# Attention sums kept in DRAM with 32 rows a head, and a resident bias

## The chip, the cores and the metric

The kernel runs on one core of a Trainium2 chip. The time is the device time of one launch in microseconds (us), and lower is better. Times before and after are medians of several runs on a chip; the rows further down are from one execution that the hardware profiler recorded.

## The reference

Two transformer layers are applied to x of 2048 tokens by 640 channels. Both layers share one set of weights. Each layer is attention with 32 heads of 20 channels over a sliding window of 256 tokens, and then a feed-forward block with a squared ReLU.

```python
def _A_ref(x, wqkv, wo):
    H = 32; Dh = D // H; W = 256
    q, k, v = split(x @ wqkv)                      # each head: 2048 x 20
    scores = jnp.einsum("bhqd,bhkd->bhqk", q, k) * (Dh ** -0.5)
    mask = (idx[:, None] - idx[None, :] >= 0) & (idx[:, None] - idx[None, :] < W)
    p = _softmax(jnp.where(mask, scores, -1e9))
    return merge_heads(jnp.einsum("bhqk,bhkd->bhqd", p, v)) @ wo

def _B_ref(x, w1, b1, w2, b2):
    r = jnp.maximum(x @ w1 + b1, 0)
    return (r * r) @ w2 + b2

for _ in range(2):
    x = x + _A_ref(_layernorm(x), A_wqkv, A_wo)
    x = x + _B_ref(_layernorm(x), B_w1, B_b1, B_w2, B_b2)
```

## The kernel before

**Units.** The tokens are cut into groups of T = 256, so that two layers make 16 units u = 0 to 15. A unit has these steps. The layer norm makes y, which is turned to channels on partitions. `stage_qk` and `stage_v` make queries, keys and values (each float32 product is three float16 products of high and low halves, `mm3`, line 339). The attention of the unit runs over eight quads of four heads. `stage_o` multiplies the divided sums by wo and adds them to x, a second layer norm follows (its y goes through TensorE transposes in unit 0 and in the last units, line 403, else through DMA transposes), and `stage_f` is the feed-forward block.

**A quad.** `max_quad` computes scores into the PSUM banks bb (line 703) and reduces them to row maxima on VectorE (lines 717, 720). `exp_quad` computes the scores again with the maxima subtracted (line 840), ScalarE takes the exponentials into pt (line 825, four of them for a quad), and GpSimd and VectorE clear the masked corners (lines 854, 863). `pv_quad` multiplies pt by the values into the tile pv and a spare piece of bb (line 931). ScalarE and VectorE bring both to the tile ot (lines 943, 946). Values carry a 21st column of ones, so each head has 20 rows of sums and one of the softmax's denominators. A quad's four heads stand at partitions 0, 32, 64 and 96 of ot.

**The way through DRAM.** After every second quad ot, which holds two quads, is written to a DRAM tile o (line 951). When a unit's eight quads are written, `load_o` reads the denominators as rs (each row four times, line 984) and the sums as val (line 985; the tiles are called od, or ov in the last two units). In four quarters of 64 tokens, VectorE takes the reciprocal of rs (line 1017) and multiplies (1020), ScalarE rounds to float16 (1024), VectorE makes the rest (1027). `stage_o` uses the result.

**The order of the work.** Nothing is scheduled by the compiler: each engine runs its own list in order. A planner in the kernel writes the lists. It keeps a clock for each engine (A is ScalarE, D VectorE, G GpSimd, S the DMA queue of SyncE), gives each posted job a cost in ns and a priority, and puts it into a list when its inputs should be ready by those costs. Dense products (`stage_qk`, `stage_v`, `stage_o`, `stage_f`) fill TensorE between the steps of the quads. Costs of DMAs thus decide where on VectorE and ScalarE the jobs behind them stand. Weights are loaded from ScalarE's queue during unit 0 and the start of unit 1 (`load_wo`, `load_w1`, `load_w2`), and split to high and low by `convert` (lines 271 and 272).

**The bias b2.** In each unit `add_b2` loads b2, spread over 128 partitions, into one of the two buffers of the pool xt (line 1069), and four additions on GpSimd add it to the unit's x (line 1076, two for each of two row blocks of 128 tokens). The layer norm of unit u + 2 loads its rows into the same pool, and waits for these additions.

Of the kernel before, what the change touches and what calls it, by code (L numbers as in the profile page):

```python
# [10 lines left out]
F32 = mybir.dt.float32  # L11
# [3 lines left out]
ALU = mybir.AluOpType  # L15

P = 128
Q = P // 2
S = 2048
D = 640  # L20
F = 1536
H = 32
DH = 20
NL = 2
T = 256
NG = S // T
NU = NL * NG
KC = D // P
# [17 lines left out]
def kernel(ctx: ExitStack, tc: tile.TileContext, x, wqkv, wo, w1, b1, w2, b2, out):  # L46
    nc = tc.nc
# [3 lines left out]
    sb = ctx.enter_context(tc.tile_pool(name="sb", bufs=1))  # L51
# [30 lines left out]
    for h in range(2):  # L82
        nc.gpsimd.tensor_copy(drop[h * Q:(h + 1) * Q], edges[h * Q:(h + 1) * Q, :, h * Q:(h + 1) * Q])
    b1s = sb.tile([P, FC], F32, name="b1s")
    kts = []
    for i in range(3):
        kts.append(sb.tile([P, NP, T], F16, name=f"kt{i}"))
# [18 lines left out]
    def set_row(i, k):  # L106
        nc.vector.memset(krow[i][:, 512 * k:512 * (k + 1)], PAIR)
# [45 lines left out]
    def bulk(fn, size, *deps, **kw):  # L153

        return post("A", 400.0, fn, *deps, prio=2, size=size, idle=True, land=WLAND, **kw)

    def dma(fn, size, *deps, n=1, cost=450.0, prio=1, **kw):

        return post("S", n * cost, fn, *deps, prio=prio, size=size, **kw)
# [107 lines left out]
    gate, gate0, gate2 = [Job("S", 0.0, None, [], 0.0, 0) for i in range(3)]  # L267
# [25 lines left out]

    def load_wo():

        v = wo.rearrange("(h c d) n -> d h c n", c=KC, d=4)
        raw = w2raw[:, (FC - KC) * D:].rearrange("p (c n) -> p c n", n=D)
        loads = []
        for d in range(4):
            loads.append(bulk(lambda d=d: nc.scalar.dma_start(raw[d * H:(d + 1) * H], v[d]), H * KC * D * 4, gate0))  # L300
        for c in range(KC):
            woj[c] = convert(raw[:, c], wo_s[:, 0, c], wo_s[:, 1, c], D, loads[-1], *loads[:-1])
        rowset[1] = [post("D", 460, lambda k=k: set_row(1, k), prio=2) for k in range(4)]
# [499 lines left out]
    ods, ots = {}, {}  # L803
# [103 lines left out]
    def pv_quad(n, quad):  # L907
        u, qd = divmod(n, NQ)
        boxes, masks = quad
        need(*pvfree)  # L910
        pvfree.clear()
        to, jobs = mm_tile([P, T], "pv")
        spare = bb6[1][:, 2, T:]
        pv = [to, spare]
        halves = quarters(u)
        for k in range(4 if halves else 2):
            need(*masks[k // 2 if halves else k])
            for j in range(2):
                for e in range(2):
                    jj = 2 * j + e  # L920
                    c = (4 * qd + jj) * (DH + 1)
                    for h in range(2 if halves else 1):
                        kb = ORDER[h][k] if halves else 2 + k
                        vf = vts[(2 * (u if kb >= 2 else u - 1) + kb % 2) % 6][1]
                        if halves:
                            o, q0, w = PARTS[h][kb]
                            r, a, b = slice(h * Q, (h + 1) * Q), (10 * j + o) * Q, (10 * j + o + w) * Q
                        else:
                            q0, w = 2 * k, 4 - 2 * k
                            r, a, b = slice(0, P), 512 * k + w * Q * j, 512 * k + w * Q * (j + 1)  # L930
                        nc.tensor.matmul(pv[h][32 * jj:32 * (jj + 1), q0 * Q:(q0 + w) * Q], vf[r, c:c + 32],  # L931
                                         boxes[e]["pt"][r, a:b], start=(k == 0), stop=(k == (3 if halves else 1)),
                                         skip_group_check=True, tile_position=(h * Q, 32 * jj))
            now[0] += (440.0, 225.0, 330.0, 305.0)[k] if halves else 420.0
        apart[0] = True
        if qd == 0:
            ods[u] = tc.dram_tile([DH + 1, H, T], F32, name=f"o{u}")
        if qd % 2 == 0:
            ots[u] = sb.tile([P, 2, T], F32, name="ot", bufs=2)
        ot = ots[u]  # L940

        def out():
            nc.scalar.copy(ot[:, qd % 2], to)  # L943

        def both():
            nc.vector.tensor_tensor(ot[:, qd % 2], spare, ot[:, qd % 2], op=ALU.add)  # L946

        def write():
            drv = ods[u].rearrange("d (q j) n -> j d q n", j=4)
            for j in range(4):  # L950
                nc.sync.dma_start(drv[j][:, qd - 1:qd + 1, :], ot[32 * j:32 * j + DH + 1])

        jobs.append(post("A", 262, out, prio=0))
        tops()
        done = jobs[-1]
        if halves:
            done = post("D", 330, both, done, prio=urgency["turn"])
            pvfree.append(done)
        if qd % 2:
            ojobs[u, qd] = dma(write, 4 * (DH + 1) * 2 * T * 4, done, n=4, cost=350.0)  # L960

    ojobs, stored, waiting = {}, [], {}

# [2 lines left out]
    ols = {}  # L966
    opened = Job("S", 0.0, None, [], 0.0, 0)

    def load_o(u, late=False, free_=()):
# [3 lines left out]
        if late:  # L973
            val = sb.tile([P, KC, T], F32, name="ov", tag="qt", bufs=2)
            od = sb.tile([P, KC, 2, T], F16, name="od", tag="yT", bufs=1)
        else:
            raw = sb.tile([P, 2, KC, T], F32, name="od", tag="hh", bufs=1)
            val = raw[:, 0]
            od = raw[:, 1].rearrange("p c n -> p (c n)").bitcast(F16).rearrange("p (c a n) -> p c a n", a=2, n=T)
        wrote = [ojobs.pop((u, qd)) for qd in range(1, NQ, 2)]  # L980
        rs = sb.tile([P, T], F32, name="rs", bufs=1)

        def load():
            nc.sync.dma_start(rs, ods[u][DH:].to_broadcast([4, H, T]))
            nc.sync.dma_start(val, ods[u][:DH].rearrange("(c d) h n -> (d h) c n", d=4))

        loaded = dma(load, P * (KC + 1) * T * 4, *wrote, *free_, n=2, prio=0)
        if u == NU - 1:
            both = sb.tile([P, 2, D], F32, name="x1", tag="qt", bufs=2)
            x1 = [both[:, i] for i in range(2)]  # L990
        elif u == NU - 2:

            x1 = [krow[(u - 1) % 3][:, i * D:(i + 1) * D] for i in range(2)]
        else:
            x1 = [sb.tile([P, D], F32, name="x1", bufs=2) for i in range(2)]
# [17 lines left out]
        for i in range(4):  # L1013
            q = slice(i * T // 4, (i + 1) * T // 4)
# [15 lines left out]
            j = post("D", 575, ratio, loaded, prio=pr)  # L1030
            j = post("D", 409, times, j, prio=pr)
            j = post("A", 360, high, j, prio=0 if i < 2 else pr)
# [32 lines left out]

    def add_b2(u):

        b2s = sb.tile([P, D], F32, name="xt", tag="xt", bufs=2)
        load = dma(lambda: nc.sync.dma_start(b2s, bass.AP(tensor=b2.tensor, offset=b2.offset, ap=[[0, P], [1, D]])),
                   P * D * 4)  # L1070
        js = []
        for i in range(2):
            for h in range(2):
                hs = slice(h * HD, (h + 1) * HD)
                js.append(post("G", 827, lambda x1=x1s[u, i], hs=hs:
                               nc.gpsimd.tensor_tensor(x1[:, hs], x1[:, hs], b2s[:, hs], op=ALU.add), load, prio=2))
        return js

    def y_cross(u):
# [287 lines left out]
    flow(todo, rest)  # L1367
    load_o(0)
    dma(lambda: nc.sync.dma_start(b1s, b1.rearrange("(c p) -> p c", p=P)), 8192, *ols[0][2], prio=2)

    while not all(j.end is not None and j.end <= now[0] + LOOK for j in bbjobs):
        c = next(rest)
# [5 lines left out]
    for u in range(1, NU):  # L1378
# [4 lines left out]
        parts, cost, ahead_ln = [], OC + FCST, u + 2 if u + 2 < NU else None  # L1383
# [45 lines left out]
```

## Time and profile before

| | before |
|---|---|
| median of 3 runs | 1559.01 us (1557.77 to 1561.9) |
| profiled execution, its own time | 1561.46 us |
| its span, first to last instruction | 1559.6 us |
| TensorE busy | 1533.5 us, 98% |
| VectorE busy | 1043.3 us, 67% |
| ScalarE busy | 669.7 us, 43% |
| GpSimd busy | 451.8 us, 29% |
| DMA queue of SyncE | 148.89 MB, 38.7% of 16 DMA engines |

The engines are called PE (TensorE's products), PEld (its weight loads, beside the products), DVE (VectorE), ACT (ScalarE), POOL (GpSimd) and SP (SyncE); SPq and ACTq are DMA issues from SP and from ACT. Where the table says 98%, TensorE had a product under way for 98% of the span. The span is shorter than the execution's own time by 1.86 us, which lie outside the first and the last instruction.

### The profile page before, as it was taken

What the parts mean: (1) busy time and instruction counts of PE and PEld (TensorE: products, weight loads), DVE (VectorE), ACT (ScalarE), POOL (GpSimd) and SP (SyncE); (2) the same over time, 40 slices, a digit from 0 to 9 for tenths busy, and PEclk for the clock granted to TensorE, in tenths of its full rate; (3) what the DMA queues carried; (4) which work ended last, traced back from release to release, by engine and by line L of the source; (5) the groups of instructions that cost most, each with busy time, mean ns of one, the idle gap of its engine ahead of it and who ended that gap; (6) DMA issues with size and microseconds to landing.
All of it is one profiled execution on the core that took longest, in us unless ns stands there. A gap on an engine that the chain in (4) does not pass through costs nothing. (4 is left out here: it accounts for less than half of the span.)

```text
span 1559.6 us, 58897 instructions
## 1 busy us (share of the span) xinstructions
PE 1533.5 (98%) x25822; PEld 1198.6 (77%) x25822; DVE 1043.3 (67%) x2244; ACT 669.7 (43%) x1365; POOL 451.8 (29%) x847
## 2 busy tenths in 40 slices
PE   8998999999999999999999999999999999999999
PEld 6666778787787877878777787877878777786777
DVE  8878775666757667675666757667675676667642
ACT  4565435334453443435343453444435335354422
POOL 1223314232141331413224141321413214142412
PEclk9999999999999999999999999999999999999999
DMA  9975354352534424344462434425243342542120
GB/s 271 209 201 127 80 121 92 106 114 54 123 88 114 105 74 126 69 126 89 99 130 63 119 91 119 100 70 132 67 126 89 94 117 65 122 90 59 30 68 18
DMA packets 248745, 162.16 MB, mean 104 GB/s; under 512 B 96552, under 2 KB 232232, under 8 KB 248488
## 3 DMA queue, kind: packets, MB, share of 16 engines
q1 hardware_dynamic: 242120, 148.89, 38.7%
q10 hardware_dynamic: 6368, 9.50, 2.1%
q8 instruction: 202, 3.31, 0.9%
q14 instruction: 55, 0.45, 0.1%
HBM read 84.68 MB, written 52.95 MB: 88 GB/s over the span
## 5 line engine op out<-in xcount | busy, mean ns | idle before, releaser
L825 ACT ACTIVATE pt<-bb 128x640 f32<-128x640 f32 (+2 forms) x512 | 311.9, 684 | 167.6 <-PE bb L840 148.9
L854 POOL TENSOR_SCALAR_AFFINE_SELECT pt<-pt 64x256 f32<-64x256 f32 x448 | 199.3, 445 | 582.1 <-ACT pt L825 560.0
L339 PE MATMUL acc<-y,w_s 128*128 128x256 f16 x2880 | 330.2, 274 | 1.2 <-DVE y L390 1.2
L339 PE MATMUL acc<-w_s,hh 128*128 128x320 f16 (+1 forms) x2340 | 326.7, 297 | 0.1
L339 PEld LDWEIGHTS <-w_s 128*128 128x128 f16 x2880 | 276.4, 98 | 40.9 <-issue 2.0
L339 PEld LDWEIGHTS <-hh 128*128 128x128 f16 x2340 | 222.1, 98 | 86.8 <-issue 0.4
L720 DVE TENSOR_REDUCE mx<-bb 128x4 f32<-128x1024 f32 x224 | 273.2, 1224 | 6.8
L339 PE MATMUL acc<-yT,wq_s 128*128 128x256 f16 x2250 | 259.1, 273 | 3.0 <-DVE qd L537 1.2
L339 PEld LDWEIGHTS <-wq_s 128*128 128x128 f16 x2400 | 229.6, 98 | 37.3 <-issue 4.3
L863 DVE COPY_PREDICATED_SCALAR pt<-drop,zero 128x256 f32 x224 | 99.9, 497 | 134.3 <-ACT pt L825 133.8
L1130 DVE TENSOR_TENSOR hh<-r,hh 128x256 f16<-128x256 f32 x192 | 98.3, 525 | 110.8 <-ACT hh L1127 105.7
L931 PE MATMUL pv<-pt,vt 64*32 64x192 f32 (+5 forms) x3840 | 166.7, 302 | 0.9 <-DVE y L390 0.6
L943 ACT COPY ot<-pv 128x256 f32<-128x256 f32 x128 | 47.6, 372 | 276.1 <-PE bb L931 247.2
L1124 POOL TENSOR_TENSOR r<-r 128x256 f32<-128x256 f32 x192 | 121.9, 655 | 127.9 <-ACT r L1120 125.3
L931 PE MATMUL bb<-pt,vt 64*32 64x128 f32 (+3 forms) x3584 | 153.5, 301 | 0.0
L717 DVE COPY_PREDICATED bb<-maskq,bb 128x256 f32<-128x256 uint16 x224 | 93.8, 423 | 85.7 <-PE bb L703 80.0
L931 PEld LDWEIGHTS pv<-pt,vt 64*32 64x32 f32 (+1 forms) x3840 | 125.5, 106 | 31.7 <-issue 3.7
L339 PE MATMUL acc<-wo_s,od 128*128 128x320 f16 x960 | 139.6, 299 | 2.2 <-ACT od L1024 2.0
L339 PE MATMUL acc<-wq_s,yT 128*128 128x320 f16 x900 | 132.1, 302 | 5.0 <-DVE qd L537 4.2
L1120 ACT ACTIVATE r<-acc,b1s 128x256 f32<-128x256 f32 x192 | 81.1, 476 | 98.6 <-PE acc L339 96.5
L339 PEld LDWEIGHTS <-od 128*128 128x128 f16 x960 | 90.9, 98 | 40.6 <-ACT od L1024 2.3
L339 PEld LDWEIGHTS <-yT 128*128 128x128 f16 x900 | 87.1, 98 | 40.0 <-issue 6.2
(103 smaller groups left out, 1476.3 us busy)
## 6 DMA issues: line engine op xcount, KB each, us to landing
qt<-qk SPq DMA_DIRECT2D x30, 480.0 KB
kt<-qk SPq DMA_DIRECT2D x30, 480.0 KB
o<-ot SPq DMA_DIRECT2D x256, 42.0 KB
qk<-qd SPq DMA_DIRECT2D x15, 640.0 KB
od<-o SPq DMA_DIRECT2D x14, 640.0 KB
qk<-yl SPq DMA_DIRECT2D x13, 640.0 KB
xt<-in_A_x_dram SPq DMA_DIRECT2D x16, 320.0 KB
x<-in_A_x_dram SPq DMA_DIRECT2D x16, 320.0 KB
```

Source lines behind the costliest of these rows:

```text
L339: nc.tensor.matmul(acc, lhs(a, c), rhs(b, c), start=(k == 0), stop=(k == 3 * nk - 1))
L717: nc.vector.copy_predicated(wins[:, :, 4 * Q:], later, wins[:, :, :Q])
L720: nc.vector.tensor_reduce(most, wins[:, :, Q:], axis=mybir.AxisListType.X, op=ALU.max)
L825: return lambda: nc.scalar.activation(room_of(box)[:, a:b], bank[:, a:b], AF.Exp, scale=SCALE / (QS * QS))
L854: nc.gpsimd.affine_select(out=m, in_=m, pattern=[[0, 4], [-1 if k else 1, Q]], base=0, fill=0.0, compare_op=ALU.is_gt if k else ALU.is_ge, ...
L863: nc.vector.copy_predicated(m, drop[:, k:k + 1, :].bitcast(mybir.dt.uint16).to_broadcast([P, 4, Q]), zero.unsqueeze(1).to_broadcast([P, 4, ...
L931: nc.tensor.matmul(pv[h][32 * jj:32 * (jj + 1), q0 * Q:(q0 + w) * Q], vf[r, c:c + 32], boxes[e]["pt"][r, a:b], start=(k == 0), stop=(k == ...
L943: nc.scalar.copy(ot[:, qd % 2], to)
L1120: nc.scalar.activation(box["r"], acc[:, f, :], AF.Relu, bias=b1s[:, f0 + f:f0 + f + 1], scale=1.0 / (YS * WS))
L1124: nc.gpsimd.tensor_tensor(box["r"], box["r"], box["r"], op=ALU.mult)
L1130: nc.vector.tensor_sub(hh[:, 1, f, :], box["r"], hh[:, 0, f, :])
```

## The change

The DRAM tile of a unit has 32 rows for each head in place of 21: head by head, 20 rows of sums, the denominator, and 11 rows that nothing reads. All 128 partitions of ot are then one piece, so a pair of quads is written by one DMA in place of four. The planner's cost for it is 600 ns in place of 4 x 350. A partition of val now holds five neighbouring channels of a head, so one piece of 5 KB in DRAM, where it held five rows of 1 KB that lay apart. The rows of wo are loaded in the matching order, which makes two DMAs of 128 partitions in place of four of 32. The bias gets a tile of its own, is loaded once in unit 0, and `add_b2` has neither a load nor a buffer from the pool xt.

```diff
@@ setup
+    b2s = sb.tile([P, D], F32, name="b2s")
@@ load_wo
-        v = wo.rearrange("(h c d) n -> d h c n", c=KC, d=4)
+        v = wo.rearrange("(p c) n -> p c n", c=KC)
...
-        for d in range(4):
-            loads.append(bulk(lambda d=d: nc.scalar.dma_start(raw[d * H:(d + 1) * H], v[d]), H * KC * D * 4, gate0))
+        for c0, n in ((0, 2), (2, 3)):
+            loads.append(bulk(lambda c0=c0, n=n: nc.scalar.dma_start(raw[:, c0:c0 + n], v[:, c0:c0 + n]), P * n * D * 4, gate0))
@@ pv_quad
-            ods[u] = tc.dram_tile([DH + 1, H, T], F32, name=f"o{u}")
+            ods[u] = tc.dram_tile([H, 32, T], F32, name=f"o{u}")
...
-            drv = ods[u].rearrange("d (q j) n -> j d q n", j=4)
-            for j in range(4):
-                nc.sync.dma_start(drv[j][:, qd - 1:qd + 1, :], ot[32 * j:32 * j + DH + 1])
+            nc.sync.dma_start(ods[u].rearrange("(q j) e n -> (j e) q n", j=4)[:, qd - 1:qd + 1, :], ot)
...
-            ojobs[u, qd] = dma(write, 4 * (DH + 1) * 2 * T * 4, done, n=4, cost=350.0)
+            ojobs[u, qd] = dma(write, P * 2 * T * 4, done, cost=600.0)
@@ load_o
-            nc.sync.dma_start(rs, ods[u][DH:].to_broadcast([4, H, T]))
-            nc.sync.dma_start(val, ods[u][:DH].rearrange("(c d) h n -> (d h) c n", d=4))
+            nc.sync.dma_start(rs, ods[u][:, DH:DH + 1].to_broadcast([H, 4, T]))
+            nc.sync.dma_start(val.rearrange("p c n -> p (c n)"), ods[u][:, :DH].rearrange("h (d c) n -> h d (c n)", d=4))
@@ add_b2
-        b2s = sb.tile([P, D], F32, name="xt", tag="xt", bufs=2)
-        load = dma(lambda: nc.sync.dma_start(b2s, bass.AP(tensor=b2.tensor, offset=b2.offset, ap=[[0, P], [1, D]])),
-                   P * D * 4)
...
-                               nc.gpsimd.tensor_tensor(x1[:, hs], x1[:, hs], b2s[:, hs], op=ALU.add), load, prio=2))
+                               nc.gpsimd.tensor_tensor(x1[:, hs], x1[:, hs], b2s[:, hs], op=ALU.add), *b2load, prio=2))
@@ after load_o(0)
+    b2load = [dma(lambda: nc.sync.dma_start(b2s, bass.AP(tensor=b2.tensor, offset=b2.offset, ap=[[0, P], [1, D]])),
+                  P * D * 4, *ols[0][2], prio=2)]
```

Since the planner's costs change, so do the lists. TensorE has the same instructions; 322 lines of 40,399 differ, all of them in unit 0 and at the start of unit 1, and from there on its order is the old one. Line numbers after the change are one higher up to line 948, and 1 to 4 lower behind that. Three places follow.

GpSimd at the start of the feed-forward block of unit 1, before (L1076 adds the bias, L1124 squares, L854 masks a quad's corners):

```order
L1076 TENSOR_TENSOR x_3400<-x_3400,xt 128x320
L1124 TENSOR_TENSOR r<-r 128x256 x2
L1076 TENSOR_TENSOR x_3400<-x_3400,xt 128x320
L854 AFFINE_SELECT pt<-pt 64x4x64 x4
L1124 TENSOR_TENSOR r<-r 128x256 x2
L1076 TENSOR_TENSOR x_3401<-x_3401,xt 128x320 x2
L1124 TENSOR_TENSOR r<-r 128x256 x4
```

And after (L1072 adds, L1120 squares, L855 masks):

```order
L1072 TENSOR_TENSOR x_3375<-x_3375,b2s 128x320 x2
L1072 TENSOR_TENSOR x_3376<-x_3376,b2s 128x320 x2
L1120 TENSOR_TENSOR r<-r 128x256 x2
L855 AFFINE_SELECT pt<-pt 64x4x64 x4
L1120 TENSOR_TENSOR r<-r 128x256 x6
```

The four additions moved ahead of the first squares and masks. The later units, up to the last, move in the same way.

ScalarE in unit 0, some 53 us after the start, before (L943 copies a quad's sums, L309 issues the first load of w1, L534 empties a PSUM bank of queries, L825 are exponentials, L271 converts a fifth of wo):

```order
L943 COPY ot<-pv 128x256
L309 DMA w_s<-in_B_w_dram 128x5x256
L534 ACTIVATE qd<-acc 128x2x256
L534 ACTIVATE qd<-acc 128x256
L825 ACTIVATE pt<-bb_142 128x512
L825 ACTIVATE pt<-bb_143 128x512
...
L271 ACTIVATE wo_s<-w_s 128x640
```

And after, at the same place (L944, L272, L535 and L826 are the same lines):

```order
L944 COPY ot<-pv 128x256
L272 ACTIVATE wo_s<-w_s 128x640 x2
L535 ACTIVATE qd<-acc 128x2x256
L272 ACTIVATE wo_s<-w_s 128x640 x2
L535 ACTIVATE qd<-acc 128x256
L826 ACTIVATE pt<-bb_143 128x512
```

The conversions of wo moved ahead of the emptying of the banks and of the exponentials, and the load of w1 behind them.

TensorE at the end of `stage_o` of unit 0, which runs beside the first quads of unit 1, before (L339 here is the product with wo, L403 are the transposes of the second layer norm's y, three and two for the first block of rows and five for the second; L703 and L840 are the score products of two quads, 38 of each):

```order
L339 MATMUL acc<-wo_s,od 128x320
L403 MATMUL tr<-ident,xt 128x128 x3
L703 LDWEIGHTS qt
L703 MATMUL bb_142<-kt_94,qt 64x256
...
L403 MATMUL tr<-ident,xt 128x128 x2
L931 MATMUL pv<-pt,vt_99 32x256
...
L403 MATMUL tr<-ident,xt 128x128 x5
L840 LDWEIGHTS kt_95
L840 MATMUL bb_142<-qt,kt_95 64x128
```

And after:

```order
L340 MATMUL acc<-wo_s,od 128x320
L404 MATMUL tr<-ident,xt 128x128 x3
L841 LDWEIGHTS kt_96
L841 MATMUL bb_143<-qt,kt_96 64x128
...
L404 MATMUL tr<-ident,xt 128x128 x2
L704 LDWEIGHTS qt
L704 MATMUL bb_143<-kt_95,qt 64x256
...
L404 MATMUL tr<-ident,xt 128x128 x5
L340 LDWEIGHTS w_s
L340 MATMUL acc<-y_2042,w_s 128x256
```

Before, the quad's line 840 stood ahead of the last 30 of the 60 products with wo; now all 60 are done before it, only two transposes stand between it and line 703 of the next quad, and after the five transposes come at once the products that need them.

## Rows read from the trace of the kernel before

**Rows 1.** Windows: length, busy per engine, granted clock, DMA share, GB/s.
```profile
100.00:120.00 20.00, 18.65 (x336) 13.60 (x336) 17.58 (x35) 13.09 (x26) 4.50 (x8) 1.00 0.68 199
120.00:140.00 20.00, 16.33 (x319) 11.34 (x317) 18.81 (x39) 9.48 (x19) 5.08 (x10) 1.00 0.69 170
140.00:160.00 20.00, 19.40 (x294) 15.89 (x295) 14.20 (x25) 11.33 (x24) 11.31 (x15) 0.83 0.16 43
...
400.00:800.00 400.00, 398.08 (x6843) 311.20 (x6841) 267.91 (x597) 169.90 (x347) 116.37 (x218) 1.00 0.42 101
...
1480.00:1540.00 60.00, 60.00 (x627) 47.70 (x626) 25.60 (x58) 20.45 (x48) 17.50 (x28) 1.00 0.14 45
```

**Rows 2.** Waits of PE: total us, times, longest.
```profile
PE acc L339 <- DVE qd L537: 5.3, 3, 4.2
PE bb L840 <- issue: 2.3, 3, 1.1
...
PE bb L886 <- DMA qt<-mT: 0.4, 1, 0.4
```

**Rows 3.** The page: DMA queue 1 (packets, MB, share), writes of o.
```profile
q1 hardware_dynamic: 242120, 148.89, 38.7%
...
o<-ot SPq DMA_DIRECT2D x256, 42.0 KB
```

**Rows 4.** Timeline of SP's DMA issues: start, us, issues.
```profile
111.99 0.51 SPq L585 DMA_DIRECT2D qk<-qd  x1
...
129.84 1.36 SPq L951 DMA_DIRECT2D o<-ot  x4
...
136.49 0.36 SPq L1069 DMA_DIRECT2D xt<-in_B_b_dram  x1
```

**Rows 5.** Waits of POOL for the bias: total us, times, longest.
```profile
POOL x L1076 <- DMA xt<-in_B_b_dram: 81.1, 12, 8.8
```

**Rows 6.** Timeline of POOL, unit 2, where the feed-forward block starts.
```profile
438.67 0.86 POOL L1076 TENSOR_TENSOR x<-x,xt 128x320 f32<-128x320 f32 x1 [8.16 <-DMA xt<-in_B_b_dram]
439.48 1.18 POOL L1124 TENSOR_TENSOR r<-r 128x256 f32<-128x256 f32 x2
```

**Rows 7.** Timeline, unit 0's last queue issues and conversions on ACT.
```profile
45.11 0.59 ACTq L300 DMA_DIRECT2D w_s<-in_A_wo_dram  x1
...
50.02 0.57 ACTq L300 DMA_DIRECT2D w_s<-in_A_wo_dram  x1
...
54.69 0.60 ACT L534 ACTIVATE qd<-acc 128x512 f16<-128x512 f32 x1 [1.35 <-PE acc L339]
...
58.48 0.76 ACT L271 ACTIVATE wo_s<-w_s 128x640 f16<-128x640 f32 x1
```

**Rows 8.** Timeline of all engines, end of unit 0's `stage_o`.
```profile
129.86 0.75 PE L840 MATMUL bb<-qt,kt 62*64 62x128 f16 x37 [1.34 <-DVE ot L946]
...
130.55 4.53 PE L339 MATMUL acc<-wo_s,od 128*128 128x320 f16 x30
...
130.75 1.30 ACT L825 ACTIVATE pt<-bb 128x640 f32<-128x640 f32 x2 [1.79 <-PE bb L840]
...
131.93 1.31 ACT L825 ACTIVATE pt<-bb 128x640 f32<-128x640 f32 x2
...
140.24 1.30 PE L403 MATMUL tr<-ident,xt 128*128 128x128 f32 x5 [1.78 <-DVE xt L378]
...
142.00 0.88 DVE L390 TENSOR_TENSOR y<-tr,y 128x384 f16<-128x384 f32 x2
142.14 1.17 PE L840 MATMUL bb<-qt,kt 62*64 62x128 f16 x31 [0.36 <-DVE mx L720]
```

**Rows 9.** Timeline of the tail: the last sums' way.
```profile
1490.32 2.05 SPq L951 DMA_DIRECT2D o<-ot  x4
...
1500.00 0.49 DVE L1020 TENSOR_TENSOR ov<-ov,rs 128x320 f32<-128x320 f32 x1 [0.87 <-DMA ov<-o]
...
1502.88 8.31 PE L339 MATMUL acc<-wo_s,od 128*128 128x320 f16 x60
```

## The prediction, as it was put on record

> **What bounds the kernel now.** I first read the windows, which give for a stretch of the span how long each engine was busy [rows 1]. From 160 us on TensorE is full: 398.08 of 400 us in the stretch shown, and 60.00 of 60 in the tail. The weak places are early. From 100 to 120 us it has 18.65 of 20, from 120 to 140 us 16.33 of 20, and in the next 20 us its granted clock is 0.83, which is a part of the stretch at 1.2 in place of 2.4 GHz after the idle time. Then I read who keeps TensorE waiting [rows 2]: VectorE emptying a bank (5.3 us in total, 4.2 of it in one wait), "issue", which is a wait that the profile doesn't explain (2.3), and of all DMAs only the row maxima, 0.4 us once. No DMA of o, rs or val and no bias addition stands among TensorE's waits. So a change of these transfers can gain only through the lists that the planner writes, and at most where TensorE has idle time.
>
> **The change part by part.**
>
> *The writes of o.* Of 256 issues 192 go [rows 3]. Four of them kept SyncE's queue for 1.36 us [rows 4]. One DMA with 256 rows of 1 KB does not occur before; the nearest row is the issue at line 585, which has 640 rows and took 0.51 us, and the lower end is the 0.36 us of a load with 128. I take 0.5, since its row count lies between. That frees 64 x (1.36 - 0.5) = 55 us of SyncE. TensorE gets from it between nothing and the 0.4 us that it waited for a DMA. I take nothing, since filler products lie over every transfer.
>
> *The bytes.* A pair of quads writes 256 KB in place of 4 x 42.0 = 168 KB, so 64 pairs write 5.8 MB more; 15 of 16 loads of b2, 320 KB each, fall away (4.9 MB). Queue 1 moves 148.89 MB in 38.7% of 1559.6 us, 247 KB for each busy us [rows 3], so the 0.9 MB more are worth 3.6 us of all DMA engines. They have room, with a share of 0.42 in the long stretch [rows 1]. Cost nothing; were all of it in the way of the early loads, 3.6 us.
>
> *The pieces of 5 KB.* The same bytes in a fifth of the pieces can only land sooner. In the tail the sums are written from 1490.32 on, the first product that VectorE makes of them comes at 1500.00 after 0.87 us of waiting, and TensorE begins with wo at 1502.88 without a wait, since the planner put feed-forward products over it [rows 9]. TensorE's order in the tail does not change, so an earlier landing gains nothing there, and a later one would show there first. Taken: nothing.
>
> *The bias.* GpSimd stood 81.1 us behind loads of b2, 12 times [rows 5]. In unit 2 it waits 8.16 us, adds for 0.86, and then starts the squares of the first two tiles [rows 6]. With a resident bias the four additions take 4 x 0.86 = 3.4 us and fit into those 8.16. Squares and masks come up to 0.9 us earlier. Nobody gains, as TensorE has no wait for GpSimd in these stretches. Without that idle time the additions ahead of the masks would cost up to 3.4 us a unit. The buffer of the pool xt that comes free lets the second rows of the next norm load earlier, and that norm is not waited for either.
>
> *The conversions of wo.* Two loads in place of four let the planner put the conversions at some 53 us, ahead of the emptying of a bank that ran at 54.69 [rows 7]. The second load carries 983 KB (three fifths of wo) and stands on ScalarE's list ahead of the place of the third of 410 KB, so it is issued by 45.11 us. At 247 KB a us it lands at 49 us. Its upper end comes from the last load of before: issued at 50.02, it was there when the first conversion ran at 58.48 without a wait, so at most 8.5 us for 410 KB, 20 us for 983, which is 65 us and 12 us late. I take it as in time (the DMA engines were just able to keep up in this stretch, and the four loads together moved the same bytes), and keep the 12 us for a rival.
>
> *The new order at the start of unit 1.* This is the term that decides. Before, line 840 of a quad is followed by 30 products with wo, 4.53 us, and under them run the quad's exponentials, from 130.75 to 133.24, 2.49 us [rows 8]. After, only two transposes stand between line 841 and line 704, which needs the banks that the exponentials read, and ScalarE's list has the cast of these two transposes ahead of the exponentials. So TensorE idles there for about 2.49 + 0.4 (my estimate for the cast and its wait) - 0.3 (the transposes) = 2.6 us. The second block's norm ends about as before, some 0.5 us after the quad's products with the values (estimate: before, 1.78 us idle with less work over it). After the five transposes now come at once the products that need them. Before, line 390 had the copies ready at 142.88, 2.64 us after the transposes began at 140.24; half of that was the lower clock and the transposes themselves, so I take 1.5 us idle. Together 4.6 us, against 1.34 + 1.78 + 0.36 = 3.5 before. Since all products with wo are done earlier, nothing else is lost: the same instructions follow. The lower clock should come as before, since the idle time ahead of it is alike. Cost +1.1 us. Bounds: all idle time there gone and with it the lower clock, which takes (1 - 0.83) x 20 = 3.4 us, so -3.5 - 3.4 = -6.9; or a second such time at the lower clock, +1.1 + 3.4 = +4.5.
>
> *Sum.* 0 + 0 + 0 + 0 + 0 + 1.1, less up to 0.4 for the one DMA wait and some tenths for calmer queues: +0.6. The profiled execution took 1561.46 us, 1559.6 of it span, and would take 1562.1. It is 2.45 us slower than the median of the runs, 1559.01, so I forecast 1559.6.
>
> **A rule against the rows.** The rows say that the four issues take 1.36 us together and that TensorE waits for none of them [rows 2, 4]. The Trainium skill (DMA: Bandwidth & Descriptors, section Rules for kernel authors) says that many small transfers should be coalesced, because under 64 KB one pays mostly overhead; the four old writes of 42 KB are such. By that rule the coalescing itself would be the gain. By the rows it is not, unless the sums' way through DRAM is on the path: that is the last rival.
>
> **The rivals.**
>
> *Faster through the new order.* The sums of unit 0 are ready sooner, nothing idles between 118 and 143 us, and the clock stays up: 1559.0 - 6.9 = 1552.1. For it speaks that VectorE, 18.81 of 20 us busy there [rows 1], gets its jobs on the sums in a tighter order. Against it: the exponentials lose their cover.
>
> *Slower through wo.* The 983 KB come late, and ScalarE, which runs in order, stands before the first conversion with the banks of TensorE behind it. It decides from 53.3 us on: each us later is about one us of TensorE idle once its two banks are full. At 4 us late, with a time at the lower clock behind it, 4 + 2 = 6: 1565. Against it speaks the 4 us of margin.
>
> *Slower through the new order.* The idle time at the start of unit 1 grows enough for twice the time at 1.2 GHz: +4.5, 1563.5.
>
> *The way through DRAM sets the pace after all.* If once a unit the landing of the last write were waited for, 16 x (2.05 - 0.5) = 25 us would go [rows 9], the 2.05 being the last write there: 1534. The 60.00 of 60 us in the tail speaks against it. So does the list of waits. The Trainium skill's coalescing rule, named above, is what speaks for it.
>
> **How the numbers follow.** About neutral, 1556.5 to 1563: 0.62. Faster through the order, 1552.1: 0.16. Slower through wo, 1565: 0.12. Slower through the order, 1563.5: 0.07. The DRAM way, 1534: 0.03. A measurement of this kernel can tell about 0.3%, 4.7 us, from no change (the three runs of before spread over 4.1 us). Faster by more than that, below 1554.3: 0.16 + 0.03 = 0.19. Slower by more, above 1563.7: 0.12, and half of the 0.07, 0.16 in round numbers. Within it: 0.65. The range from 1552.5 to 1565.5 leaves out the DRAM way, about half of the faster case and less than half of the slower one, 0.17.
>
> **What would show it.** Right: in the windows the stretches from 160 us on as full as before; SyncE's write issue at 0.4 to 0.6 us; no wait of GpSimd for b2; in the stretch from 120 to 150 us a wait of line 704 for an exponential of 2 to 3 us and one of line 340 for the copies of y; a granted clock below 1 there once. Wrong: a wait of ScalarE at the first conversion of wo for its load (slower), no idle time on TensorE between 118 and 143 us and a clock of 1.00 (faster), or a stretch behind 200 us whose length has changed by over 1 us, which none of my terms allows.

## The result, and the profile after

The changed kernel takes 1566.11 us (median of 6 runs, 1563.88 to 1569.13) against 1559.30 us of the kernel before beside it (6 runs, 1557.77 to 1561.90). The ratio is 1.0044, 95% interval 1.0032 to 1.0056: slower, 6.8 us by the medians, where +0.6 was forecast. The forecast range ended at 1565.5.

The profiled execution of after is the fastest of its six, 1563.88 us with a span of 1562.0. Its windows, which answer to [rows 1], and one more for 40 to 60 us:

```profile
40.00:60.00 20.00, 17.79 (x172) 12.85 (x169) 16.36 (x65) 10.79 (x22) 4.69 (x7) 1.00 0.57 159
100.00:120.00 20.00, 18.28 (x335) 13.52 (x336) 18.34 (x33) 12.15 (x23) 4.51 (x8) 1.00 0.77 219
120.00:140.00 20.00, 17.07 (x280) 11.99 (x270) 18.87 (x41) 10.39 (x20) 4.47 (x8) 0.97 0.62 151
140.00:160.00 20.00, 18.08 (x307) 14.33 (x305) 14.92 (x26) 9.53 (x21) 9.65 (x15) 0.86 0.19 56
400.00:800.00 400.00, 398.47 (x6830) 311.85 (x6828) 267.00 (x597) 169.41 (x346) 116.14 (x218) 1.00 0.41 100
1480.00:1540.00 60.00, 60.00 (x632) 48.13 (x630) 24.62 (x56) 21.51 (x51) 17.86 (x31) 1.00 0.12 41
```

In the stretches from 160 us on TensorE's busy time changed by less than 1 us. The loss is early: from 40 to 60 us TensorE is busy 17.79 us, where before had 19.14:

```profile
40.00:60.00 20.00, 19.14 (x191) 13.68 (x189) 15.39 (x67) 8.60 (x18) 4.41 (x10) 1.00 0.98 216
```

From 120 to 160 us it has 35.15 instead of 35.73. The clock is below 1.00 in two windows now (0.97 and 0.86), and the loss is 0.03 x 20 + 0.14 x 20 = 3.4 us, as much as before had. But it fell twice. These windows of 1 us from after hold the four edges; in between the clock is 0.50, which is 1.2 GHz, and from 143 to 145 us it is 1.00:

```profile
138.00:139.00 1.00, 0.42 (x6) 0.25 (x9) 0.97 (x4) 0.80 (x2) 0.73 (x1) 0.81 0.00 0
142.00:143.00 1.00, 0.31 (x24) 0.15 (x8) 1.00 (x2) 0.37 (x1) 1.00 (x2) 0.98 0.00 0
145.00:146.00 1.00, 1.00 (x9) 0.80 (x8) 0.97 (x4) 0.73 (x2) 0.37 (x1) 0.73 0.01 3
148.00:149.00 1.00, 1.00 (x7) 0.71 (x6) 0.51 (x1) 0.00 (x0) 0.00 (x0) 0.57 0.24 46
```

Worked out from these rows, TensorE ran at 1.2 GHz from about 138.6 to 142.0 us and from about 145.5 to 148.9 us. In before the same kind of windows show one stretch, from 139.9 to 146.9 us. So this execution shows 2.4 us more of span and no more loss of clock. The other five runs took 1.3 to 5.3 us longer than it, and the slowest two are those with the lowest clock: 0.994 and 0.993 over the whole run, where the profiled one has 0.997.

The waits of PE, which answer to [rows 2]:

```profile
PE acc L340 <- DVE qd L538: 5.9, 5, 4.2
PE bb L704 <- ACT pt L826: 3.5, 4, 2.3
PE acc L340 <- DVE y L391: 2.1, 2, 1.2
...
PE bb L841 <- issue: 1.8, 3, 0.8
PE bb L887 <- DMA qt<-mT: 1.5, 2, 1.2
```

Three grew most: L704 for exponentials (1.1 us in before) and L340 for the copies of y (1.2 in before), which were forecast, and L887 for the row maxima by DMA, 1.5 us instead of 0.4, which was not. The timeline at the last of them (PE, and SP's issues of the queries):

```profile
45.14 0.88 SPq L590 DMA_DIRECT2D qt<-qk  x2
...
48.17 0.27 PE L887 MATMUL bb<-qt,kt 62*128 62x256 f16 x1 [1.23 <-DMA qt<-mT]
48.69 0.49 PE L887 MATMUL bb<-qt,kt 62*128 62x256 f16 x7 [0.26 <-DMA qt<-mT]
```

And the timeline at the first two, which answers to [rows 8]:

```profile
134.72 0.91 PE L841 MATMUL bb<-qt,kt 62*64 62x128 f16 x38
...
135.56 0.44 PE L404 MATMUL tr<-ident,xt 128*128 128x128 f32 x2
...
136.03 0.37 ACT L390 CAST y<-tr 128x256 f16<-128x256 f32 x1 [0.73 <-PE tr L404]
136.30 1.90 ACT L826 ACTIVATE pt<-bb 128x640 f32<-128x640 f32 x3
...
138.25 0.27 PE L704 MATMUL bb<-kt,qt 60*64 60x256 f16 x1 [2.26 <-ACT pt L826]
...
138.85 1.28 PE L704 MATMUL bb<-kt,qt 60*64 60x256 f16 x37 [0.33 <-ACT pt L826]
...
141.80 3.56 POOL L1072 TENSOR_TENSOR x<-x,b2s 128x320 f32<-128x320 f32 x4
141.86 1.15 DVE L379 TENSOR_SCALAR xt<-x,bmv 128x640 f32<-128x640 f32 x1 [0.45 <-POOL bmv L377]
...
143.16 0.74 PE L404 MATMUL tr<-ident,xt 128*128 128x128 f32 x5 [0.85 <-DVE xt L379]
...
144.83 3.44 PE L340 MATMUL acc<-y,w_s 128*128 128x256 f16 x18 [0.94 <-DVE y L391]
```

The exponentials start only behind the cast at 136.03, and L704 stands 2.26 us. GpSimd's additions of the bias begin at 141.80, and VectorE's scaling of the norm beside them takes 1.15 us. Before it took 0.60:

```profile
139.49 0.60 DVE L378 TENSOR_SCALAR xt<-x,bmv 128x640 f32<-128x640 f32 x1
```

The transfers, from the page of the profile, from timelines of SP, POOL and ACT, and from the tail ([rows 3, 4, 6, 7, 9] have before):

```profile
q1 hardware_dynamic: 236824, 149.74, 38.1%
...
o<-ot SPq DMA_DIRECT2D x64, 256.0 KB
```

```profile
130.75 0.38 SPq L950 DMA_DIRECT2D o<-ot  x1
```

```profile
431.91 3.34 POOL L1072 TENSOR_TENSOR x<-x,b2s 128x320 f32<-128x320 f32 x4
439.64 1.19 POOL L1120 TENSOR_TENSOR r<-r 128x256 f32<-128x256 f32 x2 [4.40 <-ACT r L1116]
```

```profile
53.79 1.37 ACT L272 ACTIVATE wo_s<-w_s 128x640 f16<-128x640 f32 x2
```

```profile
1501.61 0.49 DVE L1019 TENSOR_TENSOR ov<-ov,rs 128x320 f32<-128x320 f32 x1
```

A write takes SP 0.38 us, the additions of unit 2 are done before the squares, the conversion of wo waits for nothing, nor does the first product with the sums in the tail. All of that is as forecast.

### The profile page after: what moved, and what is told of

It is laid out like the page before. It is cut to its first block, busy times and chain, and to the rows that moved or that the text cites. A ratio compares the mean times of both kernels' runs of the same rounds, so it can differ in the third digit from the quotient of the medians.

```text
span 1562.0 us, 58516 instructions
## 1 busy us (share of the span) xinstructions
PE 1533.2 (98%) x25822; PEld 1198.0 (77%) x25822; DVE 1036.3 (66%) x2244; ACT 669.7 (43%) x1365; POOL 454.1 (29%) x847
## 5 line engine op out<-in xcount | busy, mean ns | idle before, releaser
L826 ACT ACTIVATE pt<-bb 128x640 f32<-128x640 f32 (+2 forms) x512 | 312.4, 683 | 168.4 <-PE bb L841 151.0
L855 POOL TENSOR_SCALAR_AFFINE_SELECT pt<-pt 64x256 f32<-64x256 f32 x448 | 198.3, 443 | 597.5 <-ACT pt L826 575.7
L340 PE MATMUL acc<-y,w_s 128*128 128x256 f16 x2880 | 330.6, 274 | 2.3 <-DVE y L391 2.1
L340 PE MATMUL acc<-w_s,hh 128*128 128x320 f16 (+1 forms) x2340 | 326.7, 297 | 0.1
L340 PEld LDWEIGHTS <-w_s 128*128 128x128 f16 x2880 | 276.4, 98 | 42.2 <-issue 3.2
L340 PEld LDWEIGHTS <-hh 128*128 128x128 f16 x2340 | 222.1, 98 | 86.8 <-issue 0.4
L340 PE MATMUL acc<-yT,wq_s 128*128 128x256 f16 x2250 | 259.1, 273 | 2.9 <-DVE qd L538 1.2
L340 PEld LDWEIGHTS <-wq_s 128*128 128x128 f16 x2400 | 229.6, 98 | 37.6 <-issue 4.6
L1120 POOL TENSOR_TENSOR r<-r 128x256 f32<-128x256 f32 x192 | 122.7, 660 | 214.6 <-ACT r L1116 212.0
L932 PE MATMUL pv<-pt,vt 64*32 64x128 f32 (+5 forms) x3840 | 168.4, 304 | 1.5 <-ACT vt L623 0.9
L944 ACT COPY ot<-pv 128x256 f32<-128x256 f32 x128 | 47.7, 372 | 283.6 <-PE bb L932 246.5
L1126 DVE TENSOR_TENSOR hh<-r,hh 128x256 f16<-128x256 f32 x192 | 90.5, 485 | 108.9 <-ACT hh L1123 104.5
L932 PE MATMUL bb<-pt,vt 64*32 64x192 f32 (+3 forms) x3584 | 154.9, 302 | 0.0
L340 PE MATMUL acc<-wo_s,od 128*128 128x320 f16 x960 | 139.3, 299 | 2.0 <-ACT od L1023 2.0
L340 PE MATMUL acc<-wq_s,yT 128*128 128x320 f16 x900 | 131.6, 301 | 5.3 <-DVE qd L538 4.5
L340 PEld LDWEIGHTS <-od 128*128 128x128 f16 x960 | 91.0, 98 | 40.3 <-ACT od L1023 2.3
L340 PEld LDWEIGHTS <-yT 128*128 128x128 f16 x900 | 86.8, 98 | 40.2 <-issue 6.9
```

The lines of the kernel that those rows point to most:

```text
L340: nc.tensor.matmul(acc, lhs(a, c), rhs(b, c), start=(k == 0), stop=(k == 3 * nk - 1))
L826: return lambda: nc.scalar.activation(room_of(box)[:, a:b], bank[:, a:b], AF.Exp, scale=SCALE / (QS * QS))
L855: nc.gpsimd.affine_select(out=m, in_=m, pattern=[[0, 4], [-1 if k else 1, Q]], base=0, fill=0.0, compare_op=ALU.is_gt if k else ALU.is_ge, ...
L1120: nc.gpsimd.tensor_tensor(box["r"], box["r"], box["r"], op=ALU.mult)
L1126: nc.vector.tensor_sub(hh[:, 1, f, :], box["r"], hh[:, 0, f, :])
```

## The experiments

The theories. **A**: the new order of unit 1's start costs, by idle time and by the clock that falls after it. **W**: the loads of wo in bigger pieces hold up the small rows of qt. **C**: the additions of the resident bias slow VectorE's norm. **B**: the new transfers of o cost by themselves. Every ratio below is to runs of the kernel before beside it on the same chip, with its 95% interval.

**e1 to e4: undoing parts of the change.**

```diff
e1, e2  -  ojobs[u, qd] = dma(write, P * 2 * T * 4, done, cost=600.0)
        +  ojobs[u, qd] = dma(write, 4 * (DH + 1) * 2 * T * 4, done, cost=1400.0)
e1, e3  -  for c0, n in ((0, 2), (2, 3)):  one load of raw[:, c0:c0 + n]
        +  for d in range(4):  one load of raw[d * H:(d + 1) * H] from v[d * H:(d + 1) * H]
e4      +  add_b2 loads b2 for each unit into the pool xt, as before; no b2s
```

> The changed kernel with two edits undone: the output weights load in four DMAs of 32 partitions (in the permuted rows), and the planner is told the old size and cost of a write of o (1400 ns). TensorE's and VectorE's instruction lists are then those of the kernel before, to the row; the one write per pair of quads, the 5-KB pieces, the permuted rows and the resident bias stay. Theory A (the loss comes from the new order, by idle time and clock between 40 and 150 us): 1559 us, ratio 0.999 to 1.001. Theory B (the loss comes from the transfers or the bias themselves): it keeps 1566, ratio 1.004. If only part comes back, 1561 to 1564, both hold.

Measured: 1563.34 us, 1.0012 (1.0003 to 1.0020). Most of the loss went with the order, as A said, but not all. Two places show what stayed. At 47 us L887 waits 0.36 and 1.84 us for the rows of qt, and SP's two issues of the queries take 2.70 us:

```profile
45.44 2.70 SPq L590 DMA_DIRECT2D qt<-qk  x2
```

```profile
49.30 0.49 PE L887 MATMUL bb<-qt,kt 62*128 62x256 f16 x7 [1.84 <-DMA qt<-mT]
```

And at 141.79 VectorE's scaling takes 1.18 us beside the additions that GpSimd began at 140.95. The transposes behind it wait 2.37 us, where before had 1.78:

```profile
141.79 1.18 DVE L379 TENSOR_SCALAR xt<-x,bmv 128x640 f32<-128x640 f32 x1
143.12 0.73 PE L404 MATMUL tr<-ident,xt 128*128 128x128 f32 x5 [2.37 <-DVE xt L379]
```

The Trainium skill (SBUF — State Buffer, section SBUF: two separate sides) says that VectorE, in its two-port modes or with two inputs in SBUF, and GpSimd share a pair of ports, and that one of them waits for the whole instruction of the other. The trace agrees in direction: 1.18 beside an addition, 0.60 without. No run shows the ports themselves.

> The changed kernel, but the planner is told the old size and cost of a write of o; the output weights stay in two DMAs. Its TensorE list differs from that of before in rows 1033 to 3697, another order than either. Theory A1 (the price is the order in which stage_o of unit 0 meets unit 1's exponentials, which the write's cost moved): idle of some 4 us at 128 to 142 us as before, 1559 to 1561. Theory A2 (the price is the load of wo in two DMAs with what it moves at 40 to 60 us): stays at 1564 to 1567. Theory B: stays at 1566.

Measured: 1565.82 us, 1.0028 (1.0018 to 1.0039). This third order has other waits from 120 to 160 us (2.4 us for the norm, 1.8 for ot, 1.3 for the values), and keeps a wait of 1.43 us at 47 us. A2 predicted the time better than A1, but as its order is neither of the two, it doesn't part them.

> The changed kernel, but the output weights load in four DMAs of 32 partitions as before (in the permuted rows); the planner's new cost of a write stays. Its TensorE list is that of before up to row 2032 and from row 4269 on. Theory A2 (wo in two DMAs): 1559 to 1561, and the idle of 1.23 us at 46.9 us is back at 0.4. Theory A1 (the write's cost and the order of unit 1's start): stays at 1563 to 1567. Theory B: stays at 1566.

Measured: 1576.25 us, 1.0098 (1.0083 to 1.0113), a miss of every theory. Its order brings waits further on: from 160 to 215 us the longest waits of PE are

```profile
PE bb L704 <- ACT pt L826: 2.4, 2, 2.1
PE bb L841 <- DVE mx L721: 1.7, 1, 1.7
PE bb L704 <- DMA kt<-qk: 1.2, 1, 1.2
```

where after has none in this stretch longer than 0.1 us. This order costs more than any of the edits.

> The changed kernel, but b2 loads for each unit into a shared tile as before; TensorE's and VectorE's lists are those of the changed kernel to the row. Theory A: the same as the changed kernel, 1566, ratio 1.003 to 1.006. Theory B with the resident bias as the cause: 1559 to 1561.

Measured: 1567.20 us, 1.0032 (1.0018 to 1.0046), as theory A said. GpSimd waits for the loads of b2 again, 62.0 us in 10 waits, but not in unit 0, where the additions still run beside VectorE's scaling (1.14 us). TensorE's waits are those of the changed kernel (L704's line number is 703 here, again with 3.5 us).

**e5 to e8: the parts by themselves.**

```diff
e5  before, with  + b2s, one load of b2 after load_o(0), no load in add_b2
e6  e1, with      + for c in range(d, d + 1 if d < 3 else KC):
                  +     nc.scalar.dma_start(raw[:, c], v[:, c])
e7  e6, with      + the additions of unit 0 posted with wait=2000.0
e8  after, with   + if n == 13: spin(8)      # ahead of the products of L704 that wait 2.26 us
```

The call spin(n) puts n products of the identity, which nothing needs, into TensorE's list as a filler.

> The kernel before, with the resident bias alone (one load of b2 behind unit 0's o, the adds no longer wait for a load of their own). TensorE's, VectorE's and ScalarE's lists are those of before; POOL's adds for unit 0 move up to just behind the second power of the norm. Theory C (POOL's add beside VectorE's scaling of the norm makes it 1.18 us where it was 0.60, and the products behind it wait: 2.37 and 1.00 us idle where before had 1.78 and 0.36): 1.2 us of idle more than before, ratio 1.001. Theory D (the loss of e1 lies in the load of wo alone): ratio 1.000, the scaling at 0.60 us.

Measured: 1561.23 us, 1.0005 (0.9996 to 1.0013). The scaling takes 1.19 us and the transposes wait 2.37, as theory C has it. In the time, 0.6 us more of waiting is not to be told from nothing.

> The kernel of e1 (the change with TensorE's and VectorE's order of before), but wo loads by columns of rows: three loads with 2560 bytes a partition and one post with two such loads, so pieces of 2560 bytes instead of 12.8 KB, with the same bytes. Theory W (big pieces hold up the small rows of qt at 43 to 49 us): the idle at 47 us falls from 2.20 us to below 0.8, as before, and the two issues of qt from 2.70 to about 1.1 us; the span falls by 1.2 to 1.5. Theory W2 (the late rows come from the number of bytes or of loads): the idle at 47 us stays at 1.5 to 2.2.

Measured: 1561.39 us, 1.0000 (0.9990 to 1.0010). SP's two issues take 0.89 us, and from 40 to 62 us PE waits for nothing, as theory W said. The edit has a second side that this run doesn't part from the size of a piece: the loads are five with 128 partitions each, where e1 has four with 32.

```profile
46.32 0.89 SPq L594 DMA_DIRECT2D qt<-qk  x2
```

> e6, and POOL's adds of the resident bias for unit 0 are posted 2 us later, so that the mask of the next quad stands ahead of them, as before. Theories W and C together: the layout of o, the single writes and the resident bias are all there and cost nothing: 1559 to 1561, ratio 0.999 to 1.000, idle at 140 us 1.8 and 0.4 as before. If the new transfers of o cost something themselves (theory B): ratio 1.001 to 1.002.

Measured: 1559.41 us, 0.9988 (0.9978 to 0.9998). The scaling is at 0.60 us again, as the addition now runs at 146.35. With the new transfers of o and the resident bias in place the time is no longer than before's, so theory B falls.

```profile
138.11 0.60 DVE L383 TENSOR_SCALAR xt<-x,bmv 128x640 f32<-128x640 f32 x1
```

> The changed kernel with eight products of the identity put into TensorE's list ahead of the products of L704 that wait 2.26 us for the exponentials (2.0 us by 1.73 for seven at the start of the program); all other lists are those of the changed kernel. Their result is not used. Theory K (the clock's fall is a part of the price): the stretch 120 to 160 us is at 2.4 GHz for longer, the span falls by 1.7 to 3.4 us. Theory I (only the idle time counts): the time stays at that of the changed kernel within 0.5 us, since the idle is only filled.

Measured: 1562.47 us, 1.0012 (1.0002 to 1.0023), against 1.0038 of the changed kernel (e9). Eight useless products in a wait won 4 us; theory I fell. What they changed is the clock (the windows are e8's; the changed kernel's second profiled execution stands under e9):

```profile
120.00:140.00 20.00, 19.24 (x286) 13.77 (x284) 19.04 (x42) 10.29 (x20) 3.29 (x6) 1.00 0.67 148
140.00:160.00 20.00, 17.09 (x348) 13.94 (x351) 16.25 (x29) 9.99 (x23) 10.84 (x17) 1.00 0.24 70
```

```profile
139.56 0.27 PE L706 MATMUL bb<-kt,qt 60*64 60x256 f16 x1 [0.25 <-ACT pt L828]
```

L704 (here L706) still starts when its exponentials are ready. But the clock is 1.00 in both windows, and over the 12 runs the granted clock is 0.9968 in the mean, where the changed kernel's 5 runs have 0.9946. That is (0.9968 - 0.9946) x 1562 = 3.4 us of the 4. The changed kernel's six runs of the result have 0.9953, by which it would be 2.3 us.

**e9 to e12: order and pieces crossed, and the order alone.**

```diff
e10  after, with   + for c in range(c0, c0 + n): nc.scalar.dma_start(raw[:, c], v[:, c])
e11  before, with  + the new size and cost=600.0 of a write (four are still issued)
                   + for d0, n in ((0, 2), (2, 3)): two old loads of 32 partitions in each post
e12  e7, with      + spin(6) ahead of the five transposes that wait for the norm
```

> The changed kernel once more, beside the others of this call on one chip, so that the parts can be set against it. Expected ratio 1.003 to 1.005, span less lost clock about 1557, granted clock near 0.995.

Measured: 1567.97 us, 1.0038 (1.0024 to 1.0051). Its profiled execution lost 0.26 x 20 = 5.2 us of clock in the last of these windows:

```profile
140.00:160.00 20.00, 18.33 (x322) 14.06 (x322) 13.63 (x25) 9.41 (x20) 10.64 (x17) 0.74 0.24 68
```

> The changed kernel, but each of wo's two posts issues one load for each row of a partition (two, then three, of 2560 bytes a partition) instead of one load with 5 and 7.7 KB in a piece; all orders are those of the changed kernel, POOL's adds too. Theory W: the idle at 46.9 us falls from 1.23 to about 0.4 and the time by 1 to 2 us against the changed kernel, ratio 1.002 to 1.003; what is left is the order of unit 1's start. If the order alone is the price: the time stays at the changed kernel's, 1.0035 to 1.0045.

Measured: 1565.61 us, 1.0025 (1.0014 to 1.0035), in the range of theory W, but the interval overlaps e9's. The wait at 47 us is 0.74 us, where e9 has 1.03 and 0.28, and the profile puts it down to VectorE and no longer to the rows. Yet over the window from 40 to 60 us TensorE is busy 18.27 us, and 18.24 in e9:

```profile
47.99 0.49 PE L891 MATMUL bb<-qt,kt 62*128 62x256 f16 x7 [0.74 <-DVE bmv L375]
```

> The kernel before with the order of the changed one and nothing else of it: the planner is told the new size and cost of a write of o and two posts for wo, but four writes with the old rows, four loads of wo with their old pieces, the old pieces of o and a load of b2 for each unit are issued. TensorE's and VectorE's lists are those of the changed kernel. Theory A (order): idle 2.3 and 0.9 us at 136 and 144 us, a time at 1.2 GHz in 120 to 160 us in most runs, 1562 to 1565, ratio 1.001 to 1.003. If the order costs nothing: 1.000.

Measured: 1568.88 us, 1.0050 (1.0038 to 1.0063), more than theory A had room for. The order alone, without any of the new transfers, is at least as slow as the whole change (1.0038 in e9; the intervals overlap). One thing besides the order differs from before: two old loads of wo are issued in one post. Part of the loss is again at 47 us, where the rows were late, and from 40 to 60 us the clock is 0.91, as in e1, where before and after have 1.00:

```profile
50.26 0.80 PE L890 MATMUL bb<-qt,kt 62*128 62x256 f16 x7 [2.12 <-DMA qt<-mT]
40.00:60.00 20.00, 16.84 (x148) 12.09 (x147) 13.49 (x59) 8.25 (x17) 2.89 (x6) 0.91 0.78 161
```

Since these loads have the old pieces of 2560 bytes, the size of a piece is not the only thing that holds up the rows. That the number of bytes queued at that moment counts too is argued and not shown.

> e7 with six products of the identity ahead of the five transposes that wait 1.78 us for the norm at 137 us (1.48 us by 1.73 for seven); all other lists are those of e7, the products' result is not used. Theory K: fewer runs with a time at 1.2 GHz behind 137 us, 1557 to 1559, ratio 0.998 to 0.999. If the clock does not fall there in most runs of e7 anyway: the same as e7, 0.9988.

Measured: 1556.17 us, 0.9968 (0.9955 to 0.9980). The idle 1.78 us ahead of the transposes is 0.25, and the clock is 1.00 in both windows:

```profile
120.00:140.00 20.00, 17.65 (x329) 12.47 (x327) 19.11 (x39) 9.12 (x19) 4.42 (x9) 1.00 0.55 152
140.00:160.00 20.00, 19.06 (x345) 16.49 (x348) 15.93 (x29) 13.01 (x28) 14.04 (x20) 1.00 0.15 50
```

**e13 to e16: is the gain the change's own?**

```diff
e13  before, with  + v = wo.rearrange("(h c d) n -> c d h n", c=KC, d=4); load raw[:, c] from v[c]
e14  before, with  + spin(6) at the place of e12
e15  e7, e16  e12, both unchanged
```

> The kernel before with one edit: wo, in its old order of rows, loads by row of a partition (128 partitions of 2560 bytes; five loads in the four posts) instead of 32 partitions of five such pieces a load. All instruction lists but ScalarE's issues are those of before. If the gain of e7 over before comes from where wo's loads stand against the small rows at 47 us (idle 0.62 us there in before, none in e7): ratio 0.999 to 0.9995. If it comes from the new transfers of o: 1.000.

Measured: 1567.65 us, 1.0040 (1.0027 to 1.0053), a miss. The rows of qt were late three times, up to 2.98 us:

```profile
PE bb L890 <- DMA qt<-mT: 6.1, 3, 3.0
```

The pieces are those of e6, but one issue took 0.54 us (median of five) where e6's took 0.39. The source's outermost dimension is 4 here and 128 in e6. The Trainium skill (DMA: Bandwidth & Descriptors, section Why a DMA increments its semaphore by 16 and not by 1) says that a transfer goes to as many of the 16 engines as divide the outermost sizes of both sides, which would be 4 here. No run shows the number of engines, so this cause is argued and not shown, and the experiment doesn't answer what it was to answer.

> The kernel before with six products of the identity ahead of the five transposes that wait 1.78 us for the norm at 138 us, and nothing of the change. If the filler's gain in e12 has nothing to do with the change (theory K): about 0.998 here too, so that e12 stands some 0.001 below it. If before's clock falls for its other waits as well: 0.999 to 1.000.

Measured: 1560.59 us, 0.9993 (0.9985 to 1.0002). The clock is up (0.9982 in the mean of 12 runs, before 0.9965), which is worth 2.7 us, but the time is only 1 us down.

> e7 once more, beside the two variants of before in this call: 0.998 to 0.9995 if its gain is one of the kernel, 1.000 if it was chance.

Measured: 1559.82 us, 0.9988 (0.9979 to 0.9998), as in e7.

> e12 once more: 0.996 to 0.998; against e14 the gain that the change itself brings once the order, the pieces of wo and the place of the bias's adds are put right: 0.001 by e7.

Measured: 1556.19 us, 0.9966 (0.9953 to 0.9979), as in e12. So the gain is the kernel's: with the filler the change is 4.4 us faster than before with the same filler (e16 against e14), without it 1.8 us faster than before (e15). In e7's profile 0.6 us of this stand in the window from 40 to 60 us, where TensorE is busy 19.77 us (before 19.14). Where the rest comes from stays open: the waits called "issue" behind 160 us, 1.0 us in e7 and 2.3 in before, are 2.8 us in e15, the same kernel as e7.

## Why the prediction was wrong

**The step that failed** is in the new order at the start of unit 1: "The lower clock should come as before, since the idle time ahead of it is alike." The idle time there was sized well: 2.6 + 0.5 + 1.5 = 4.6 us forecast, 2.26 + 0.33 + 0.85 + 0.94 = 4.38 measured. That the sum fits so well is partly luck, since the last two parts, 0.85 for 0.5 and 0.94 for 1.5, are off in opposite directions. The clock was not as before. In e9's comparison its mean is 0.9946, and 0.9967 in the runs of before, worth 0.0021 x 1562 = 3.3 us of the 6.2; with the six runs of the result (0.9953) the changed kernel has 0.9950, worth 2.6 us. The rival "slower through the new order" had this, with +4.5 for a second time at 1.2 GHz, and held 0.07 of the chance. The clock did fall a second time in the profiled execution, but for as long in all as in before, so only the granted clock of many runs shows the loss. The other 3 us or so are time that TensorE lost without a lower clock, by standing idle: e8 has the clock of before (0.9968, before 0.9966 in the same comparison) and still takes 1.0012 of its time.

How much of the clock belongs to the new order is not shown. Filling a wait gives the old order 3.6 us as well (e15 to e16), so the 4 us of e8 are not the price of the new order alone. And part of what differs lies elsewhere: from 20 to 40 us the clock is 0.91 in before and in after, and 0.83 in e9, which is the same program as after:

```profile
20.00:40.00 20.00, 15.29 (x119) 11.01 (x117) 15.23 (x41) 5.99 (x11) 2.02 (x2) 0.83 0.92 235
```

The crossed experiments give the order's price in time:

| ratio to before | old order | new order |
|---|---|---|
| wo in big pieces | 1.0012 (e1) | 1.0038 (e9) |
| wo in pieces of 2560 bytes | 1.0000 (e6) | 1.0025 (e10) |

It is 0.0025 in both rows, 3.9 us, each with an uncertainty of some 2 us. Not all else is equal: a big piece is 12.8 KB in e1 and 5 or 7.7 KB in e9, and the new order issues the loads of wo in two posts. In the second row the mean clocks are alike (0.9957 in e6, 0.9960 in e10), so there the price is idle time, and much of it lies ahead of unit 1, from 40 to 60 us:

```profile
40.00:60.00 20.00, 19.77 (x198) 14.24 (x197) 16.31 (x72) 8.46 (x19) 4.56 (x10) 1.00 0.90 197
40.00:60.00 20.00, 18.27 (x177) 13.13 (x178) 17.17 (x69) 10.90 (x22) 5.38 (x9) 1.00 0.63 172
```

The first line is e6's, the second e10's. So the new order costs, by the clock and by idle time; the shares of the two stay open.

**A second step was missing.** The terms for the bytes ("Cost nothing") and for the pieces ("can only land sooner") looked at o and b2 alone. For wo I asked only whether its own conversions would be late. They weren't (no wait at 53.79), and the rival "slower through wo" did not happen. But wo's loads run beside the small rows of qt, which TensorE waits for, and these came late: L887 waited 1.5 us instead of 0.4, and TensorE's busy time from 40 to 60 us fell by 1.35 us. The columns of the table put the pieces at 0.0012 and 0.0013, about 2 us, each with an interval that reaches zero. In the old order the traces agree with it (17.61 us busy from 40 to 60 in e1, 19.77 in e6); in the new order they don't (18.24 and 18.27). The 0.4 us of [rows 2] for the row maxima was the sign for it; I read it as a bound on a gain and not as a wait that could grow.

**A third was mis-sized.** The bias was taken as nothing, since GpSimd had idle time for the additions. It has, but for unit 0 they moved beside VectorE's scaling, which went from 0.60 to 1.18 us, with TensorE waiting for it. By e5 that is at most 0.0013, by e6 against e7 0.0012, with intervals that overlap.

**What was right.** The wait of line 704 for exponentials (2 to 3 us forecast, 2.26 measured) and the one of line 340 for the copies of y. The write's issue (0.5 forecast, 0.38 measured, and nothing of it on the path). The bytes of queue 1 (0.9 MB more forecast, 0.85 measured) at no cost. The tail, full at 60.00 of 60. GpSimd's wait for b2 gone. No stretch behind 200 us that moved by a microsecond. The coalescing rule of the Trainium skill, weighed in the prediction, gave none of the 25 us that it would have been worth: none of TensorE's waits in before was for these writes.

**The sum as measured.** Order 3.9, wo's pieces 2.0 and the bias up to 1.9 make 5.9 to 7.8 us; e7 shows that without them the change is 1.8 us faster than before. Together 4.1 to 6.0, where the medians give 6.8 in the result and 6.2 in e9 (interval 3.7 to 8.0). Every term is uncertain by some 2 us, so the sum agrees with the time and proves no term.

The fastest version measured keeps every transfer of the change, in the old order, with wo loaded by rows of 2560 bytes, the additions of unit 0 after the next masks and six products as filler: 1556.2 us, 0.9966 of before.

## What to carry to other kernels

Where a planner turns costs into an order, an edit that changes a cost changes the program: give the planner the old cost first and look at the edit alone, since orders here moved the time by 0.25% to 1% and the edits by some 0.1%. Price an idle stretch of TensorE by its length and by the clock that may fall behind it, and take the granted clock from many runs, as one profile doesn't show how often it happens. If a wait can't be removed, useless products in it can be worth it (4 us for 2 us of them in e8, but 1 us in e14). And ask of every large transfer which small one, waited for, is under way at the same time.

## What the runs showed of the hardware that was not expected

- In after the clock fell to 1.2 GHz at about 138.6 us, behind one wait of 2.26 us, was back at 142.0 and fell again at about 145.5, behind waits of 0.85 and 0.94. Of the 14 profiled executions without a filler 13 lost clock between 138 and 155 us (e7 did not, e15, the same kernel, did); of the four with one (e8, e12, e14, e16) none did. The Trainium skill (TensorE: Matmul & The Clock Gate, section Why this matters for your kernels) advises against long idle gaps between bursts of products; the trace agrees in kind, with a gap of 2.26 us.
- The same program's granted clock varies from 0.993 to 0.997 between runs (after, six runs), and its time with it by 5.3 us.
- A float32 scaling of 128 x 640 on VectorE takes 0.60 us alone and 1.15 to 1.19 beside additions on GpSimd.
- Beside loads of wo with 12.8 KB in a piece and 32 partitions on ScalarE's queue, two issues on SyncE's queue took 2.70 us; beside loads with 2560 bytes and 128 partitions 0.89 (e1, e6).
